# Three expert blocks: the first layer of 512 tokens from Strassen's products of 256, in place of plain matmuls of 512

## The chip, the cores and the metric

The kernel runs on 1 core of one Trainium2 chip. The metric is the device time of one execution in microseconds (us), as a median of runs. The core has five engines that work side by side: TensorE (PE, with the weight loads shown apart as PEld), VectorE (DVE), ScalarE (ACT), GpSimd (POOL) and SyncE (SP), which here only issues DMAs. PE writes its results into 8 PSUM banks.

## What is computed

Three layers in a row, on 2 x 576 = 1152 tokens of 512 features. The reference, cut to what matters here:

```python
scores = scale * q @ k.T + decay, causal; attn = softmax(scores); x = attn @ v   # B=2, H=8, S=576, D=64
p = domain_probs / domain_probs.sum(-1)
for e in range(4):                                # experts, 512 -> 1024 -> 512
    h = np.maximum(x @ w1[e], 0.0)
    out += p[:, e:e + 1] * (h @ w2[e])
h = out @ w_in                                    # MLP, 512 -> 2048 -> 512, weights in float64
return (h * (1.0 / (1.0 + np.exp(-1.702 * h)))) @ w_out
```

## The kernel before

Every fp32 matrix product is made of three matmuls in a faster 32-bit format: each operand is split into a rounded part (hi) and the rest (lo), and hi·hi, lo·hi and hi·lo are added in PSUM. The split of a weight tile (`split_w`, L212) is one operation on ACT (`whi`, through L60) and one on DVE (`wlo`, L230); the split of a result of the first layer is a relu and rounding on ACT and a subtraction on DVE or POOL.

The work is cut into visits: a visit is one block of 512 hidden units (blocks 0 to 7 are halves of the four experts, 8 to 11 quarters of the MLP) on some tokens. The list is made at L145 to L147. Visits 0 to 6 run beside attention on its chunks of tokens; visits 7 to 9 (from `v_exp`) are blocks 3, 1 and 0 on tokens 512 to 1151; visits 10 to 13 (from `v_all`) are blocks 4 to 7 on all tokens; visits 14 to 17 (from `v_mlp`) are the MLP's blocks. Tokens come in groups: `EXP[0]` and `EXP[1]` (E0 and E1 below) are two of 320 tokens, `REST` is the first 512, and `MLP` is three of 384.

The first layer (L1) of a visit has two forms. The plain one (`emit_l1`, kind 1 in the list `seq`) makes four groups of 12 matmuls, over all the group's tokens at once. The joint one (`emit_joint`, kind 3) takes two groups of tokens of the same size as the two columns of a 2 x 2 block product and needs 7 products instead of 8 (Strassen's scheme in Winograd's form), in two halves (m = 0 and 1) of 7 steps, each step one product of 6 matmuls with the moving size of one group. Its operands are sums of weights and of tokens that have splits of their own: `sum_weights` (L243, 4 operations on POOL of 256 columns), `high_sums` and `low_sums` (`sh` on ACT, `sl` on DVE, two of 512 columns each, or both in `split_sums`), and `sum_tokens` (L290) for E0 and E1 or the MLP's groups. A product's result is combined with others on DVE in `first_part` (ACT), `second`, `third`, `third_out`, `fourth`, `fifth`, `plain_out` and `plain_low` (L929 to L963); some of these outputs go through the tile `jc` (2 buffers), ACT's relu and rounding, and POOL's subtraction (`output`, L907). The product named s4 adds into the same bank that `third_out` reads. The second layer (L2, kind 2) makes one tile of 128 tokens per step, 12 matmuls of 512 columns, and DVE adds it to the accumulator (L1049). REST's second layer takes its tiles in the order 3, 0, 1, 2.

For blocks 4 to 7 the list gives, per visit: joint half E0, then L2 of REST of the visit before, joint half E1, L1 of REST (plain, kind 1, moving size 512), L2 of E0 (five tiles).

The order of the work is written out by hand in a loop over `seq` (L1228 to L1318). Each step emits its matmuls, then the evacuation of the step before, then due splits (`split_next`), then what `place` (L1190) has put at that step, then steps of the conversion of the MLP's weights, at a rate (`cv_due`, L1307). ACT, DVE and POOL are held to this order (`pin_turn`, L1141); PE is held to it only up to the joint halves of the first visit on all tokens (L1313), and otherwise may take what is ready. `place` places weight sums and splits for visits 8 to 10 only; for later visits the sums follow the splits of their own weights.

The MLP's weights come in float64. `mlp_convert` (L349) turns each of 32 tiles into float32 with one ACT and six DVE operations, one per step of the generator (192 steps); SP stores each to DRAM (`wm`), and SP loads them again in pairs for `split_w`. The weights of the second layer use two pools of four buffers in turn (`wb_p` and `late["wb"]`).

## Time and profile before

| | us |
|---|---|
| median of 3 runs | 692.34 (692.19 to 693.61) |
| the profiled execution, whole | 693.89 |
| its span, first to last instruction | 692.2 |
| busy in it: PE / PEld / DVE / ACT / POOL | 681.9 / 596.3 / 505.4 / 341.7 / 222.3 |

The rows further down come from the one profiled execution. A timeline row gives the start, the time of the row, the engine, the line of the kernel, the operation, and what it writes and reads; x4 says that four like instructions are drawn together. The time of one matmul in a row holds its way through the array, so that rows overlap; what a matmul costs in a stream is the distance from start to start. Where an engine was idle before an instruction, the brackets give for how long and what ended it.

### The profile page before, as it was taken

How to read it: one execution, taken by the hardware profiler on the slowest of the kernel's cores; microseconds unless marked ns; L12 is line 12 of the kernel's file. 1: busy time of each engine (PE TensorE's matmuls, PEld its weight loads, DVE VectorE, ACT ScalarE, POOL GpSimd, SP SyncE). 2: the span in 40 equal slices, each digit the busy share in tenths (PEclk: the TensorE clock that was granted, in tenths of full speed). 3: DMA queues.
4: the chain of work that ended last, by engine and by line, in shares of the span. 5: the costliest groups of instructions: out<-in, count | busy, mean ns of one | idle time of the engine just before them, and what ended most of it. 6: DMA issues, size and time to landing. Idle time of an engine off the chain costs nothing.

```text
span 692.2 us, 10730 instructions
## 1 busy us (share of the span) xinstructions
PE 681.9 (99%) x3829; PEld 596.3 (86%) x3829; DVE 505.4 (73%) x1057; ACT 341.7 (49%) x789; POOL 222.3 (32%) x266
## 2 busy tenths in 40 slices
PE   8998999999999999999999999999999999999997
PEld 4787888888988998898888888888899998998986
DVE  6886677766569678686876788777699798786632
ACT  5768677666532735734334344343457462551420
POOL 6877576532133554515105114112004202200000
PEclk9999999999999999999999999999999999999999
DMA  7696636341312144142422452344132244221012
GB/s 258 224 303 236 232 122 242 92 118 73 104 48 65 58 122 147 52 137 78 140 103 82 148 152 78 121 152 143 56 107 76 77 157 158 81 93 45 1 46 91
DMA packets 38597, 83.37 MB, mean 120 GB/s; under 512 B 3560, under 2 KB 3568, under 8 KB 38544
## 3 DMA queue, kind: packets, MB, share of 16 engines
q1 hardware_dynamic: 38504, 82.65, 36.1%
q8 instruction: 30, 0.49, 0.3%
q14 instruction: 23, 0.19, 0.1%
q10 hardware_dynamic: 40, 0.04, 0.0%
HBM read 71.88 MB, written 10.78 MB: 119 GB/s over the span
## 4 chain that ended last, share of the span: by engine, by line
PE 94%; DMA 2%; POOL 1%; DVE 1%; ACT 1%; issue 0%; SPq 0%; POOLq 0%; ACTq 0%
PE m L1016 43%; PE m L866 20%; PE m L904 19%; PE s L587 4%; PE x L691 4%; PE t L661 3%; DMA wst<-in_wa_moe_dram 1%; PE m L1161 1%; DMA dpraw<-in_dp_dram 1%; POOL ks L513 0%; PE m L883 0%; POOL e L643 0%; PE t L735 0%; PE m L1077 0%; POOL qlo L531 0%
## 5 line engine op out<-in xcount | busy, mean ns | idle before, releaser
L1016 PE MATMUL m<-whi,hh 128*128 128x512 f32 x432 | 121.7, 392 | 0.0
L1016 PE MATMUL m<-whi,hl 128*128 128x512 f32 x432 | 119.6, 390 | 0.0
L1016 PE MATMUL m<-wlo,hh 128*128 128x512 f32 x432 | 119.2, 390 | 0.0
L230 DVE TENSOR_TENSOR wlo<-wst,whi 128x512 fp32r<-128x512 f32 x140 | 105.2, 767 | 7.6 <-ACT whi L60 7.1
L1016 PEld LDWEIGHTS m<-wlo,hh 128*128 128x128 f32 x432 | 80.9, 188 | 16.9
L1016 PEld LDWEIGHTS m<-whi,hl 128*128 128x128 f32 x432 | 80.9, 188 | 16.8
L60 ACT ACTIVATE whi<-wst 128x512 fp32r<-128x512 f32 x144 | 85.4, 625 | 17.3 <-DMA wst<-in_wa_moe_dram 7.4
L1016 PEld LDWEIGHTS m<-whi,hh 128*128 128x128 f32 x432 | 79.5, 188 | 13.9
L914 POOL TENSOR_TENSOR hl<-jc,hh 128x320 fp32r<-128x320 f32 x42 | 39.6, 945 | 156.5 <-ACT hh L60 151.6
L251 POOL TENSOR_TENSOR sr<-wst 128x256 f32<-128x256 f32 x20 | 18.1, 903 | 150.0 <-DVE tl L306 47.8
L866 PE MATMUL m<-xh,whi 128*128 128x256 f32 (+2 forms) x304 | 64.3, 327 | 0.3 <-DVE hl L1005 0.3
L866 PE MATMUL m<-xh,wlo 128*128 128x256 f32 (+2 forms) x304 | 64.3, 325 | 0.0
L866 PE MATMUL m<-xl,whi 128*128 128x256 f32 (+2 forms) x304 | 63.9, 326 | 0.0
L643 POOL TENSOR_SCALAR e<-e,sm 128x128 f32<-128x128 f32 (+4 forms) x72 | 45.5, 642 | 54.9 <-DVE sm L641 29.0
L912 ACT ACTIVATE jc<-jc 128x320 f32<-128x320 f32 x42 | 19.7, 469 | 75.3 <-DVE jc L910 75.3
L1049 DVE SCALAR_TENSOR_TENSOR acc<-m,dpn,acc 128x512 f32<-128x512 f32 x63 | 46.6, 744 | 11.0 <-PE m L1016 11.0
L866 PEld LDWEIGHTS m<-xh,whi 128*128 128x128 f32 x304 | 50.4, 189 | 3.8 <-DVE hl L1005 0.6
L866 PEld LDWEIGHTS m<-xh,wlo 128*128 128x128 f32 x304 | 50.6, 189 | 2.5
L866 PEld LDWEIGHTS m<-xl,whi 128*128 128x128 f32 x304 | 50.2, 189 | 2.6
L633 ACT ACTIVATE e<-e,mx 128x128 f32<-128x128 f32 (+4 forms) x72 | 41.6, 581 | 12.2 <-DVE mx L617 11.5
L999 ACT ACTIVATE m<-m 128x384 f32<-128x384 f32 x48 | 23.0, 479 | 35.6 <-DVE m L910 33.1
L931 ACT ACTIVATE u<-m 128x320 f32<-128x320 f32 (+1 forms) x20 | 9.0, 451 | 62.7 <-PE m L904 62.7
(141 smaller groups left out, 1326.3 us busy)
## 6 DMA issues: line engine op xcount, KB each, us to landing
wst<-in_wa_moe_dram SPq DMA_DIRECT2D x28, 512.0 KB, 3.7
wst<-in_wb_moe_dram SPq DMA_DIRECT2D x28, 512.0 KB, 4.2
mst<-in_wa_mlp_dram SPq DMA_DIRECT2D x16, 512.0 KB, 4.0
wm<-wf SPq DMA_DIRECT2D x32, 256.0 KB, 3.4
mst<-in_wb_mlp_dram SPq DMA_DIRECT2D x16, 512.0 KB, 3.8
wst<-wm SPq DMA_DIRECT2D x16, 512.0 KB, 3.6
cb<-cumd SPq DMA_DIRECT2D x16, 256.0 KB, 3.9
qr<-in_qk_dram SPq DMA_DIRECT2D x8, 384.0 KB, 5.2
```

What stands on the lines that cost most here:

```text
L60: return nc.scalar.activation(out=out, in_=in_, func=AF.Copy)
L230: (nc.gpsimd if v_ == 0 and kind == 'a' and g < 4 else nc.vector).tensor_sub(lf, raw, f(hf))
L587: nc.tensor.matmul(pt[:, :z - a], lhsT=lr[i][0], rhs=lr[i][1], start=i == 0 and not (both and pt is not bank), stop=i == n - 1, skip_group ...
L633: nc.scalar.activation(out=e[:, off:off + w], in_=e[:, off:off + w], func=AF.Exp, scale=-1.0, bias=mx, accum_out=sm[:, 0, k:k + 1])
L643: nc.gpsimd.tensor_scalar(out=e[:, off:off + w], in0=e[:, off:off + w], scalar1=sm[:, 0, i:i + 1], scalar2=1.0, op0=ALU.mult, op1=ALU.mult)
L691: nc.tensor.matmul(pt[64 * g:64 * g + 64, o:n], lhsT=lhsT, rhs=rhs, start=i == 0, stop=i == nk - 1)
L866: nc.tensor.matmul(p[:, :n], lhsT=w[:, k, :], rhs=x[c][:, k, :], start=(j == 0 and k == 0), stop=(j == 2 and k == 3))
L904: nc.tensor.matmul(p[:, :WN], lhsT=w[a][:, k, :], rhs=x[z][:, k, :], start=start and j == 0 and k == 0, stop=stop and j == 2 and k == 1, s ...
L914: nc.gpsimd.tensor_sub(hl[:, g, :], r, f(hh[:, g, :]))
L999: nc.scalar.activation(out=p[:, :n], in_=p[:, :n], func=AF.Gelu_apprx_sigmoid)
L1016: nc.tensor.matmul(p, lhsT=h_tile(v_, b, c, j, x, k), rhs=wb[v_, k][w].rearrange("p a c -> p (a c)"), start=i == 0 and k == 0, stop=i == 2 ...
L1049: nc.vector.scalar_tensor_tensor(out=a, in0=p, scalar=d, in1=a, op0=ALU.mult, op1=ALU.add)
```

## The change

For blocks 5, 6 and 7 (`both_joint`, visits 11 to 13) REST's first layer is made by the joint form too, on chunks 0 and 1 of the attention, 256 tokens each (unit kind 7, two halves of 7 steps). The order in these visits becomes E0, L2 of REST of the visit before, 7/0, E1, 7/1, L2 of E0. The token sums for this are made and split during attention (`rest_sums`, three steps of a generator per step of the main loop), stored to DRAM, and loaded into the memory of the second pool of second-layer weights in block 4 (`load_rest_sums`, on POOL's queue); the second-layer weights of blocks 4 to 11 then have one pool. The joint form gets two orders of its evacuations (`tight`, `held`), and E1's half the order of products that visits 7 to 9 use in it. Weight sums, their splits and the weights' splits are placed at fixed steps for visits 11 to 13, PE is held to program order in them, REST's L2 goes through its tiles in the order 0, 1, 2, 3, and the conversion has other rates: none in joint units, 2 to 3 a step in L2 units, and 1.75 instead of 1.3 in the MLP.

```diff
+    both_joint = range(v_all + 1, v_mlp)
...
+        if v_ in both_joint:
+            seq += [(3, v_, b, cs[0])] + before + [(7, v_, b, 0), (3, v_, b, cs[1]), (7, v_, b, 1), (2, v_, b, cs[0])]
+            before = [(2, v_, b, REST)]
+            continue
...
-        p = wa_p if kind == "a" else late["wb"] if late and v_ % 2 else wb_p
+        p = wa_p if kind == "a" else wb_p
...
-    placed = range(v_exp + 1, v_all + 1)
+    placed = range(v_exp + 1, v_mlp)
...
+    def rest_sums():
...
+        def split(n, r, o):
+            t = room.tile([128, 2, SA], F32R, tag="rs", name="rs")
+            round_act(t[:, 0], r)
+            yield
+            nc.vector.tensor_sub(t[:, 1], r, f(t[:, 0]))
+            yield
+            nc.sync.dma_start(out=tsd[:, :, n - 1, o].rearrange("x p n -> p x n"), in_=f(t))
+            yield
...
+        for o in range(2):
+            yield from total(ra, o, (sub_, h12, h11), (add_, ra, l12), (sub_, ra, l11))
+            yield from split(1, ra, o)
+            yield from total(rb, o, (sub_, h22, ra), (add_, rb, l22))
+            yield from split(2, rb, o)
+            yield from total(ra, o, (sub_, rb, h21), (sub_, ra, l21))
+            yield from split(4, ra, o)
+            yield from total(rb, o, (sub_, h22, h12), (add_, rb, l22), (sub_, rb, l12))
+            yield from split(3, rb, o)
...
+    def load_rest_sums():
+        for t, src in zip(tsr, tsd):
+            nc.gpsimd.dma_start(out=t, in_=src.rearrange("p n k c -> p n (k c)"))
...
-    def emit_joint(v_, b, m):
-
-        c1, c2 = visits[v_][1][:2]
+    held = []
+
+    def emit_joint(v_, b, m, ts, c1, c2):
+
         WN = span[c1][1]
-        late_sums = m == 1 and len(visits[v_][1]) == 2
+        tight = v_ in both_joint and (c1 == 0) != m
+        late_sums = m == 1 and (v_ < v_all or v_ in both_joint and c1 == EXP[0])
...
+                while held:
+                    held.pop()()
...
-                yield both_(third_out, fourth)
+                yield third_out if tight else both_(third_out, fourth)
                 product(pa, a12, ts[21], False, True)
-                yield both_(plain_out, plain_low)
+                yield both_(plain_out, fourth if tight else plain_low)
...
-                yield both_(fourth, plain_low)
+                yield fourth if tight else both_(fourth, plain_low)
             product(pc, s4, ts[22], False, True)
-            yield fifth
+            yield both_(fifth, plain_low) if tight else fifth
...
-        if c == REST:
-            j = (3, 0, 1, 2)[j]
...
+        for v_ in range(v_all, v_mlp):
+            b, (c1, c2, _) = visits[v_]
+            h0, h1, l2 = (3, v_, b, c1), (3, v_, b, c2), (2, v_, b, c1)
+            more = v_ + 1 in both_joint
+            if v_ == v_all:
+                mid = (1, v_, b, REST)
+                put(h1, 0, load_rest_sums)
+                put(h0, 1, sum_weights, v_ + 1, 0)
+                put(mid, -0.5, high_sums, v_ + 1, 0)
+                put(mid, 0, low_sums, v_ + 1, 0)
+                put(mid, 1, sum_weights, v_ + 1, 1)
+                continue
+            r0, r1 = (7, v_, b, 0), (7, v_, b, 1)
+            put(r0, 5.5, high_sums, v_, 1)
+            put(h1, -0.5, low_sums, v_, 1)
+            if more:
+                put((2, v_ - 1, b - 1, REST), 2, sum_weights, v_ + 1, 0)
+                put(h1, 1, sum_weights, v_ + 1, 1)
+                put(r1, 6, high_sums, v_ + 1, 0)
+                put(l2, 0, low_sums, v_ + 1, 0)
+            fill = (2, v_ - 1, b - 1, REST)
+            for k, (u, i) in enumerate([(fill, 3), (fill, 3), (r0, 0), (r0, 1)]):
+                put(u, i, split_w, "b", v_, k)
+            for g in range(4):
+                put(l2, g, split_w, "a", v_ + 1, g)
...
+            if rest_gen and not late:
+                for _ in range(3):
+                    next(rest_gen[0], None)
...
-                    cv_due[0] += ((0.75 if kind == 4 else 0) if v_ < v_all else 1.4 if b < NMOE else 1.3) * (4 / n_steps)
+                    if v_ in both_joint and v_ + 1 in both_joint or v_ + 1 == v_mlp and c != REST or v_ == v_all and kind == 2 and c == REST:
+                        rate = 0 if kind != 2 else 11 / 4 if c == REST else 2
+                    elif v_ == v_all:
+                        rate = {3: 0, 1: 1.25, 2: 3.25}[kind]
+                    else:
+                        rate = (0.75 if kind == 4 else 0) if v_ < v_all else 1.4 if v_ == v_all else 1.75
+                    cv_due[0] += rate * (4 / n_steps) if rate != 11 / 4 else 3 * (g < 3)
...
-                pinned = v_ < v_all or v_ == v_all and kind == 3
+                pinned = v_ < v_all or v_ == v_all and kind == 3 or v_all <= v_ < v_mlp and u in pin_units
```

## Rows read from the trace of the kernel before

**Rows 1.** The page: busy time and share by engine; the last chain by engine.

```profile
PE 681.9 (99%) x3829; PEld 596.3 (86%) x3829; DVE 505.4 (73%) x1057; ACT 341.7 (49%) x789; POOL 222.3 (32%) x266
...
PE 94%; DMA 2%; POOL 1%; DVE 1%; ACT 1%; issue 0%; SPq 0%; POOLq 0%; ACTq 0%
```

**Rows 2.** Busy time by windows: attention's last part, blocks 5 to 7, the MLP.

```profile
core 0: us, PE busy (x) PEld busy (x) DVE busy (x) ACT busy (x) POOL busy (x), PEclk, DMA share, GB/s
140.00:200.00 60.00, 60.00 (x416) 51.27 (x415) 34.81 (x103) 35.30 (x97) 14.98 (x26) 1.00 0.28 91
200.00:217.30 17.30, 17.30 (x89) 15.72 (x88) 16.78 (x24) 6.06 (x11) 6.14 (x6) 1.00 0.19 62
337.80:480.80 143.00, 143.00 (x720) 124.50 (x719) 108.65 (x204) 54.77 (x119) 34.66 (x38) 1.00 0.37 122
510.00:650.00 140.00, 140.00 (x706) 126.92 (x705) 112.97 (x192) 67.63 (x136) 19.75 (x20) 1.00 0.27 92
```

**Rows 3.** Timeline, PE: starts of matmuls of 256, 320 and 512 columns.

```profile
131.60 0.64 PE L866 MATMUL m<-xl,whi 128*128 128x256 f32 x4
...
133.52 0.39 PE L1016 MATMUL m<-whi,hh 128*128 128x512 f32 x1
...
339.54 0.46 PE L904 MATMUL m<-th,sh 128*128 128x320 f32 x2
...
341.30 0.46 PE L904 MATMUL m<-th,whi 128*128 128x320 f32 x2
...
373.76 1.07 PE L1016 MATMUL m<-whi,hl 128*128 128x512 f32 x4
...
376.48 0.39 PE L1016 MATMUL m<-whi,hl 128*128 128x512 f32 x1
```

**Rows 4.** Groups by line and shape: busy us, mean ns | idle before.

```profile
L1049 DVE SCALAR_TENSOR_TENSOR acc<-m,dpn,acc 128x512 f32<-128x512 f32 x63 | 46.6, 744 | 11.0 <-PE m L1016 11.0
L914 POOL TENSOR_TENSOR hl<-jc,hh 128x320 fp32r<-128x320 f32 x42 | 39.6, 945 | 156.5 <-ACT hh L60 151.6 <-issue 4.8
L251 POOL TENSOR_TENSOR sr<-wst 128x256 f32<-128x256 f32 x20 | 18.1, 903 | 150.0 <-DVE tl L306 47.8 <-DVE sl L266 38.7 <-DMA wst<-wm 23.6
L1005 DVE SCALAR_TENSOR_TENSOR hl<-m,hh 128x256 fp32r<-128x256 f32 x32 | 13.5, 421 | 6.0 <-ACT hh L1004 5.5
L934 DVE TENSOR_TENSOR u<-m,u 128x320 f32<-128x320 f32 x14 | 6.8, 484 | 3.6 <-issue 2.6 <-ACT hh L60 0.7 <-PE m L904 0.2
```

**Rows 5.** Timeline, POOL: weight sums one behind the other.

```profile
281.90 0.74 POOL L251 TENSOR_TENSOR sr<-wst 128x256 f32<-128x256 f32 x1
282.61 0.73 POOL L252 TENSOR_TENSOR sr<-wst 128x256 f32<-128x256 f32 x1
```

**Rows 6.** Timeline: hand-overs from PE to DVE, and a late sum's split.

```profile
341.50 0.49 DVE L937 TENSOR_TENSOR u<-m,u 128x320 f32<-128x320 f32 x1
...
347.59 1.09 PE L1016 MATMUL m<-wlo,hh 128*128 128x512 f32 x4
347.85 1.16 ACT L60 ACTIVATE sh<-sr 128x512 fp32r<-128x512 f32 x2 [2.60 <-PE m L904]
...
348.51 1.29 DVE L266 TENSOR_TENSOR sl<-sr,sh 128x512 fp32r<-128x512 f32 x2 [3.87 <-ACT sh L60]
...
359.41 1.28 DVE L230 TENSOR_TENSOR wlo<-wst,whi 128x512 fp32r<-128x512 f32 x2
```

**Rows 7.** Waits: engine, line, what ended them; total us, times, longest.

```profile
PEld m L904 <- DVE sl L284: 0.2, 1, 0.2
```

**Rows 8.** DMA issues: the store and the reload, KB each, median us to landing.

```profile
wm<-wf SPq DMA_DIRECT2D x32, 256.0 KB, 3.4
...
wst<-wm SPq DMA_DIRECT2D x16, 512.0 KB, 3.6
```

**Rows 9.** Timeline, DVE: two of the conversion's six operations.

```profile
340.22 0.68 DVE L368 SCALAR_TENSOR_TENSOR wf<-mst,cvt 128x512 uint32<-128x512 uint32 x1
...
340.94 0.43 DVE L371 TENSOR_SCALAR cvt<-wf 128x512 uint32<-128x512 uint32 x1
```

More of the change, by code (lines that the diff above doesn't have):

```diff
@@ L36, with __init__, __getitem__ @@
 WARM, FILL = 11, (4, 3, 3, 2, 2, 2, 3, 3,)
+class Halves:
+    def __init__(self, *parts):
+        self.parts = parts
+    def __getitem__(self, at):
+        p, k, n = at
+        return self.parts[k // 2][p, k % 2, n]
 @with_exitstack
@@ L216, in split_w @@
         raw = raw_w.pop((kind, v_, g))
-        p = wa_p if kind == "a" else late["wb"] if late and v_ % 2 else wb_p
-        hi = p.tile([128, 4, 128], F32R, tag="hi", name="whi")
-        lo = p.tile([128, 4, 128], F32R, tag="lo", name="wlo")
+        p = wa_p if kind == "a" else wb_p
+        if kind == "b" and v_ in (v_exp, v_exp + 2):
+            hi, lo = (t[:, g].rearrange("p (a c) -> p a c", a=4) for t in tsr)
+        else:
+            hi = p.tile([128, 4, 128], F32R, tag="hi", name="whi")
+            lo = p.tile([128, 4, 128], F32R, tag="lo", name="wlo")
         hf = hi.rearrange("p a c -> p (a c)")
@@ L424, in begin_late, with view @@
         late["cd"] = pool("cd", 1)
[L425 removed]
+        late["wb"] = pool("wb2", 1)
         late["rs"] = pool("rs", 1)
[L427 removed]
+        h2 = tuple(late["h2"].tile([128, 4 * WN], F32R, name=n) for n in ("hh2", "hl2"))
+        def view(ts_, o, k, n):
+            return tuple(t[:, o:o + k * n].rearrange("p (k n) -> p k n", k=k) for t in ts_)
+        hbuf[0] = view(h2, 0, 4, WN)
+        rest_h.append(view(h2, 0, 4, SA))
+        rest_h.append(tuple(Halves(*t) for t in zip(view(h2, 4 * SA, 2, SA), view(h_t, 8 * JN, 2, SA))))
+        tsr.extend(late["wb"].tile([128, 4, 512], F32R, name=n) for n in ("tsh", "tsl"))
         acc.append(late["rs"].tile([128, 4, 512], F32, name="acc1"))
@@ L914, in output @@
                 nc.gpsimd.tensor_sub(hl[:, g, :], r, f(hh[:, g, :]))
+            if b >= NMOE:
+                evac_l1(v_, b, c, g, r)
+            elif hold:
+                held.append(rest)
             else:
-                evac_l1(v_, b, c, g, r)
+                rest()
         def half(m):
@@ L923, in half @@
             if late_sums:
-                pa, pc, _, pe, pb, pd = (ps_tile() for _ in range(6))
+                pa, pc = ps_tile(), ps_tile()
+                if v_ < v_all:
+                    ps_tile()
+                pe, pb, pd = (ps_tile() for _ in range(3))
+                if v_ >= v_all:
+                    pb, pc = pc, pb
             else:
@@ L1173, in steps @@
             return len(tiles(c)) - OVER
-        return {1: 4, 2: len(tiles(c)), 3: 7, 4: 10 - OVER, 5: OVER, 6: OVER}[kind]
+        return {1: 4, 2: len(tiles(c)), 3: 7, 4: 10 - OVER, 5: OVER, 6: OVER, 7: 7}[kind]
     split_q = []
     def split_next():
+        if late and not lo_due and pair_due:
+            pair_due.pop()()
         split_rest()
@@ L1223, in attn_moe_mlp @@
     place_at = place()
+    pin_units = [u for u in seq if u[1] in both_joint and (u[1], u[3]) != (v_mlp - 1, REST)] + [u for u in seq if u[:2] == (2, v_all) and u[3] == REST]
     evac = [lambda: None]
     j_done = set()
+    rest_gen, rest_from = [], seq.index((1,) + units[6])
     cv_due = [0]
@@ L1234, in attn_moe_mlp @@
             ts_gen = sum_tokens(EXP)
-        u, m = (kind, v_, b, c), visits[v_][1].index(c)
+        if i >= rest_from and not late and ready[0] >= 1:
+            rest_gen.append(rest_gen.pop() if rest_gen else rest_sums())
+        u, m = (kind, v_, b, c), c if kind == 7 else visits[v_][1].index(c)
         if u == (1, v_mlp, NMOE, MLP[0]):
```

57 lines of the change are left out of this document (35 added, 22 removed).

## The prediction

> **What bounds the kernel now.** I read the page's busy times and its chain by engine first: PE is busy for 681.9 of 692.2 us and holds 94% of the chain that ended last [rows 1]. Then the windows: the stretch that holds blocks 5, 6 and 7 (337.8 to 480.8, from E0's half of block 5 on) is filled by PE to the last hundredth, 143.00 us at a granted clock of 1.00, while DVE has 34 us free there, ACT 88 and POOL 108 [rows 2]. So less matmul time there is less time, one for one, unless PE meets a wait that it doesn't have now. The stages on both sides, attention's last part (140 to 217.3) and the MLP (510 to 650), are filled by PE in the same way [rows 2]. DVE work moved there is free as long as DVE's free share lasts: 25 us in the 60 up to 200, 0.5 in the 17.3 behind, 27 in the MLP's 140.
>
> **What it removes: matmul time.** The price of a matmul is the spacing of starts. 12 of 512 columns take 376.48 - 373.76 = 2.72 us, 226.8 ns each; 12 of 320 take 341.30 - 339.54 = 1.76 us, 146.6 ns; 16 of 256 take 133.52 - 131.60 = 1.92 us, 120.0 ns [rows 3]. That is 0.417 ns a column and 13.4 ns fixed. The first layer of REST is now 4 x 12 = 48 matmuls of 512: 10.89 us. In the new form it is 14 products of 6 matmuls of 256: 84 x 0.120 = 10.08 us. Saved: 0.81 us a block, 2.42 us for three. The columns alone (24576 against 21504) would give 1.28 us a block; 36 more starts take 0.48 back.
> The Trainium skill says in Perfetto Trace Analysis, Optimizing Tensor Performance, Matmuls, that larger matmuls are more efficient than smaller ones. That speaks against this change, and the trace agrees by the fixed part of each start; by the rows it takes a third of the gain and not all of it.
>
> **What it adds between the products.** Each block gets 8 outputs combined from products in the place of four plain evacuations, and its weight sums and splits sit at fixed steps. Durations: a DVE add of 320 columns from PSUM 0.485, an operation of 256 0.42; POOL's subtraction of 320 0.94 (0.76 of 256 by the same ratio); an accumulation 0.74 [rows 4]; a POOL weight sum 0.74 with starts 0.71 apart when little runs beside it [rows 5]; a wlo 0.60 behind the one before (two in 1.28), a DVE add 0.20 behind the last matmul it reads [rows 6]. I put these, with the change's new order, into each engine's queue: DVE, ACT and POOL are held to program order now, and with the change PE is too in these blocks, so that no other matmul can fill a PE wait. Walking the queues of 7/0 (the first new half), E1 and 7/1 gives three waits.
> (A) The last product of 7/0, s4, adds into the bank that third_out reads, and must wait for it. It is due after six products, 6 x 0.72 = 4.32 us. On DVE stand, from the half's start: an accumulation of the L2 before (0.2 to 0.86), three wlo (2.66), second, the fourth wlo (3.6), third (4.06), third_out (4.48); with some 0.13 to PE that is 4.61: 0.3 late, three blocks: 0.9 us. Bounds 0 (one wlo less ahead of it) and 1.8 (one more short operation).
> (B) The s3 product of 7/1, in blocks 5 and 6, needs the PSUM bank that E1's plain_low gives back. From E1's start: the block's own late sums on ACT, then their two sl on DVE, which end 2.2 us behind (as now: PE begins the next work at 347.59, the second sl ends at 349.80 [rows 6]); fifth of 7/0 on DVE to 2.5, its relu and rounding on ACT to 3.4, its subtraction on POOL to 4.2; then the four weight sums of the next block, 7.1; then the subtraction of E1's third_out, 8.0. The tile jc has two buffers, so E1's fifth waits for that subtraction and ends at 8.5, plain_low at 9.0, PE starts at 9.1. It could start at 7 x 0.88 + 0.15 (wait C) + 3 x 0.72 = 8.5. 0.62 late, two blocks: 1.24 us. Queued behind that waiting fifth on DVE are plain_low, second and third. Bounds 0.4 and 1.4 a block (each sum and subtraction 0 to 0.15 longer).
> (C) E1's s4 waits for its third_out too. Its first_part stands on ACT behind the relus that 7/0 left and ends 3.7 us behind E1's start; second, third and third_out follow at 0.53 each, 5.30, and PE at 5.43; due 6 x 0.88 = 5.28. 0.15 late, three blocks: 0.45 us. Bounds 0 and 0.9.
> Such a wait is seen once now: a weight load waits 0.2 us for an sl [rows 7]. Sum of the waits 2.59 us; bounds 0.8 (B's lower end alone) and 5.5.
>
> **What it moves.** (D) REST's token sums go into attention: 44 steps, which are 28 DVE operations (x 0.42 = 12 us), 8 on ACT (3 us) and 8 stores on SP's queue from one buffer, each some 3.4 us as those of wm [rows 8]. They go three to a step while DVE has 25 us free in 60 [rows 2]; each of the 8 parts must wait for the store before it (about 8 x 4.4 = 35 us in all). If that takes them past 200, they meet a DVE that is 97% busy [rows 2]. On DVE, what waits behind them is attention's own softmax work. I take 0.2 us; bounds 0 and 1.
> (E) Loading them back is two DMAs on POOL's queue, 1 MB each, where POOL is busy for a quarter of the time and the first reader is some 30 us away: 0; 1 us if their issue held up the subtractions behind it.
> (F) The second layer's weights, with one pool where two were, are split at 7/0's first steps, behind the last L2 of the block before, which frees them. The splits are in walk A; their loads come a block ahead. 0.
> (G) REST's L2 now ends on tile 3, which the MLP's first work doesn't read: its first L1 group, 48 matmuls of 384 (0.417 x 384 + 13.4 = 173 ns each), covers the transposition for 8.3 us. 0.
> (H) Conversion of MLP weights: by the two sets of rates 85 of its 192 steps lie ahead of the MLP, where 121 do now. 36 steps of 0.55 us (half of them 0.68, half 0.43 [rows 9]) = 20 us of DVE go into the MLP's 140 us, where DVE is busy for 113 [rows 2]: 133, or 95%. A key is stored (3.4 us) and loaded again (3.6 us) before it is split [rows 8]. At the new rate, seven steps a unit where it was 5.2, the nearest case is the second pair of the fourth MLP block's first weights: its last key is made as the third block's last first-layer work begins, and its split comes 6.2 us later against 7.0. ACT, half free, would stand 0.8 us, and PE's banks hold longer than that: 0; bounds 0 and 8.
>
> **Sum.** The profiled execution is 693.89; the median of the runs, 692.34, is 1.55 lower. 693.89 - 2.42 + 2.59 + 0.2 = 694.26 for a profiled one, 692.7 as a median: the waits between the products take back what the products save.
>
> **Rivals.** This measurement can tell about 0.2%, 1.4 us, from no change.
> (1) The waits don't arise: the walk is 0.3 us too slow in DVE's queue (A and C vanish with that) and POOL takes the two subtractions before the sums, or ends them sooner (B falls to 0.4). The time is 692.34 - 2.42 + (0 to 0.8) + 0.2 = 690.1 to 690.9. For it: A and C are smaller than the error of a queue walk; blocks 5 to 7 have almost no wait today [rows 7]; DVE is a quarter free [rows 2]. Against: six products of 256 last 4.3 us where those of 320 last 5.3, with the same operations between. Chance 0.33.
> (2) Converted MLP weights come late (H). It decides at one key: if the one named there is finished one conversion later (six steps and their gaps, about 4 us), ACT stands in the split's wait with gelu and rounding queued behind it, the banks stay full, and PE loses 2 to 8 us: 695 to 700 with the rest of the sum. For it: DVE at 95%. Against: ACT is half free, and the walk has the key in time to within a microsecond. Chance 0.12.
> (3) POOL's sums run beside DVE at their mean and not at their best: 0.90 against 0.74 [rows 4, 5]. Four sums and two subtractions then end 0.85 us later in B, twice, and the time is 692.7 + 1.7 = 694.4, slower by 0.3%. It decides by what DVE does in those 3 us: with two SBUF operands (a wlo, an sl) it slows them, with PSUM operands (second, third, as beside the sums of 281.90) it doesn't. By the walk it is the latter. Chance 0.10, together with (D) at its upper bound.
> The Trainium skill, SBUF — State Buffer, SBUF: two separate sides, says that a DVE operation with two SBUF inputs and a POOL operation that reads SBUF lock each other out for the whole instruction. The two means bear out that something lengthens the sums; that it is whole instructions they don't show, 0.16 us being a quarter of one wlo.
>
> **How the numbers follow.** Forecast: 692.7, its own range 691.0 to 693.7, chance 0.45 (no change by over 0.2%). Faster by over 0.2%, rival 1: 0.33. Slower by over 0.2%, rivals 2 and 3: 0.22. The range goes from rival 1 with a little to spare, 689.8 (what the products save, with no wait and 0.1 for a start or two) to 695.5 (all waits at their upper bounds: 692.34 - 2.42 + 5.5 + 0.2 = 695.6). Rival 2's upper part is left out.
>
> **What would show it.** In the profile after: 256-wide products of L904's successor 120 ns apart, 84 in 10.1 us; PE or its weight loads waiting for third_out's add 0.1 to 0.4 us in 7/0 and E1, and for E1's plain_low 0.6 us in 7/1 of blocks 5 and 6; DVE 12 us busier in 140 to 217 without a PE gap; DVE near 133 in the MLP's 140 us, and no wait of ACT over 1 us for a wst loaded from wm. Wrong for rival 1 if PE keeps going in blocks 5 to 7, and for rival 2 if the MLP's stretch is over 1 us longer.

## The result: 7.6 us slower, and the profile after

The changed kernel takes 700.24 us (median of 4 runs, 698.43 to 701.09) against 692.67 of the kernel before beside it: a ratio of 1.0104, 95% interval 1.008 to 1.0128. The prediction was 692.7 with a range up to 695.5; the time lies outside it, on the slower side. The profiled execution's span is 698.9 us (692.2 before), its own time 700.62.

Of the page after, the line that answers to [rows 1], busy time and share by engine:

```profile
PE 684.1 (98%) x3937; PEld 600.5 (86%) x3937; DVE 533.3 (76%) x1097; ACT 352.8 (50%) x821; POOL 235.0 (34%) x286
```

PE has 108 matmuls more, as the 84 for 48 ask, and should have been busy for 2.4 us less; it is busy for 2.2 us more and idle for 4.5 more. DVE is busy for 28 us more. Where it went is read from the starts of the same work in both timelines (the first matmul of each piece):

| start of | before | after | later by |
|---|---|---|---|
| the first joint half (block 3, E0) | 217.32 | 220.02 | 2.70 |
| block 5, E0 | 337.79 | 340.31 | 2.52 |
| block 6, E0 | 385.55 | 387.96 | 2.41 |
| the first joint MLP unit | 537.54 | 539.90 | 2.36 |
| the second MLP joint visit | 585.13 | 587.46 | 2.33 |
| the third | 632.69 | 638.02 | 5.33 |
| end of the span | 692.2 | 698.9 | 6.7 |

So attention loses 2.7, the three blocks that the change is about gain 0.16 in all (2.52 to 2.36), and the MLP loses 4.3. The windows after (columns as in [rows 2]): a stretch of attention, blocks 5 to the first joint MLP unit, and from there to the end.

```profile
90.00:100.00 10.00, 7.96 (x41) 6.81 (x40) 9.59 (x30) 4.97 (x16) 8.23 (x11) 0.83 0.43 143
...
340.30:539.90 199.60, 198.97 (x1129) 179.29 (x1128) 151.79 (x258) 91.62 (x196) 52.03 (x60) 1.00 0.28 88
...
539.90:698.90 159.00, 152.43 (x757) 135.82 (x755) 118.61 (x216) 62.14 (x126) 14.47 (x16) 1.00 0.35 115
```

The same stretches in the kernel before:

```profile
90.00:100.00 10.00, 10.00 (x64) 9.01 (x63) 6.36 (x27) 6.72 (x22) 9.03 (x12) 1.00 0.37 118
...
337.80:537.50 199.70, 199.70 (x1021) 175.91 (x1020) 156.66 (x277) 85.49 (x176) 42.72 (x46) 1.00 0.34 111
537.50:692.20 154.70, 151.08 (x757) 136.25 (x756) 101.80 (x181) 59.37 (x121) 11.70 (x13) 1.00 0.24 83
```

In the ten us from 90 on PE is empty for 2.0 us, the granted clock falls to a mean of 0.83, and DVE goes from 6.36 to 9.59 busy. The timeline there (DVE and POOL, and PE where it starts again):

```profile
90.25 2.56 POOL L596 TENSOR_TENSOR qlo<-qr,qhi 64x384 fp32r<-64x384 f32 x2
91.95 1.14 DVE L362 TENSOR_TENSOR rsa<-rsa,xl 128x256 f32<-128x256 f32 x1
92.88 1.46 POOL L578 TENSOR_TENSOR ks<-kq,ks 64x576 fp32r<-64x576 f32 x1
93.01 1.62 DVE L355 TENSOR_TENSOR rs<-rsb,rs 128x256 fp32r<-128x256 f32 x1
94.88 0.14 DVE L705 TENSOR_SCALAR sm<-sm 128x1 f32<-128x1 f32 x1
...
95.01 1.22 PE L1099 MATMUL m<-whi,hh 128*128 128x512 f32 x2 [2.04 <-DVE sm L705]
```

L355 and L362 are REST's token sums (L355 the subtraction of their split). The loop emits them from 147 us on; the compiler has put them between 58 and 128. With POOL idle such an operation takes 0.41; here two take 1.14 and 1.62, and the short softmax step `sm`, queued behind them, is what PE waits for.

In 7/0, E1 and 7/1 of block 6 (DVE, POOL and PE):

```profile
409.15 0.42 DVE L980 TENSOR_TENSOR jc<-m,u 128x256 f32<-128x256 f32 x1
...
409.63 0.51 PE L974 MATMUL m<-xh,sh 128*128 128x256 f32 x2
...
415.42 0.49 DVE L980 TENSOR_TENSOR jc<-m,u 128x320 f32<-128x320 f32 x1
...
415.97 0.56 PE L974 MATMUL m<-xh,sh 128*128 128x320 f32 x2
...
417.53 1.71 POOL L985 TENSOR_TENSOR hl<-jc,hh 128x320 fp32r<-128x320 f32 x2
...
418.44 0.49 DVE L980 TENSOR_TENSOR jc<-m,u 128x320 f32<-128x320 f32 x1 [2.13 <-POOL hl L985]
418.85 0.48 DVE L1045 SCALAR_TENSOR_TENSOR hl<-m,hh 128x320 fp32r<-128x320 f32 x1
419.10 0.40 PE L974 MATMUL m<-tsh,sh 128*128 128x256 f32 x2
```

Waits A and C are there: third_out ends at 409.57, s4 starts at 409.63, 0.30 behind the end of the product before it; in E1 the same, 0.24. For wait B, the fifth of E1 does stand on DVE for 2.13 us behind POOL and plain_low ends only at 419.33, but the s3 product starts at 419.10 without waiting, while plain_low (418.85) still runs.

And in the MLP (ACT, DVE and PE; PE had no such wait there before):

```profile
603.69 0.51 PE L974 MATMUL m<-xl,sh 128*128 128x384 f32 x2
604.29 1.15 ACT L71 ACTIVATE sh<-sr 128x512 fp32r<-128x512 f32 x2 [3.63 <-PE m L974]
604.96 1.29 DVE L285 TENSOR_TENSOR sl<-sr,sh 128x512 fp32r<-128x512 f32 x2 [4.53 <-ACT sh L71]
604.98 1.14 PE L974 MATMUL m<-th,sh 128*128 128x384 f32 x4 [0.78 <-ACT sh L71]
...
643.23 0.67 ACT L418 ACTIVATE cvt<-mst 128x512 f32<-128x512 f32 x1 [9.27 <-DMA mst<-in_wb_mlp_dram]
643.80 0.47 ACT L1012 ACTIVATE u<-m 128x384 f32<-128x384 f32 x1
644.33 0.62 PE L974 MATMUL m<-xh,whi 128*128 128x384 f32 x2 [0.92 <-ACT u L1012]
```

PE waits for a late sum's split and for first_part (`u`), which stands on ACT behind a conversion's first operation that waits 9.27 us for its load.

### The profile page after: what moved, and what is told of

It is laid out like the page before. It is cut to its first block, busy times and chain, and to the rows that moved or that the text cites. A ratio compares the mean times of both kernels' runs of the same rounds, so it can differ in the third digit from the quotient of the medians.

```text
span 698.9 us, 11089 instructions
## 1 busy us (share of the span) xinstructions
PE 684.1 (98%) x3937; PEld 600.5 (86%) x3937; DVE 533.3 (76%) x1097; ACT 352.8 (50%) x821; POOL 235.0 (34%) x286
## 5 line engine op out<-in xcount | busy, mean ns | idle before, releaser
L1099 PE MATMUL m<-whi,hh 128*128 128x512 f32 x392 | 109.9, 395 | 2.6 <-DVE sm L705 2.0
L1099 PE MATMUL m<-wlo,hh 128*128 128x512 f32 x392 | 108.2, 393 | 0.0
L1099 PE MATMUL m<-whi,hl 128*128 128x512 f32 x392 | 106.7, 390 | 0.0
L985 POOL TENSOR_TENSOR hl<-jc,hh 128x320 fp32r<-128x320 f32 (+1 forms) x60 | 53.4, 891 | 144.6 <-ACT hh L71 141.4
L983 ACT ACTIVATE jc<-jc 128x320 f32<-128x320 f32 (+1 forms) x60 | 27.1, 451 | 58.9 <-DVE jc L980 58.8
L934 PE MATMUL m<-xh,wlo 128*128 128x256 f32 (+2 forms) x256 | 51.4, 314 | 0.0
L934 PE MATMUL m<-xh,whi 128*128 128x256 f32 (+2 forms) x256 | 51.1, 316 | 0.0
L934 PE MATMUL m<-xl,whi 128*128 128x256 f32 (+2 forms) x256 | 50.9, 315 | 0.0
L934 PEld LDWEIGHTS m<-xl,whi 128*128 128x128 f32 x256 | 41.1, 189 | 0.7
L418 ACT ACTIVATE cvt<-mst 128x512 f32<-128x512 f32 x32 | 21.3, 665 | 31.3 <-DMA mst<-in_wb_mlp_dram 17.4
```

Of the source, the lines that this page charges most:

```text
L418: nc.scalar.activation(out=f(t), in_=f(hi), func=AF.Abs)
L934: nc.tensor.matmul(p[:, :n], lhsT=w[:, k, :], rhs=x[c][:, k, :], start=(j == 0 and k == 0), stop=(j == 2 and k == 3))
L983: nc.scalar.activation(out=r, in_=r, func=AF.Relu)
L985: nc.gpsimd.tensor_sub(hl[:, g, :], r, f(hh[:, g, :]))
L1099: nc.tensor.matmul(p, lhsT=h_tile(v_, b, c, j, x, k), rhs=wb[v_, k][w].rearrange("p a c -> p (a c)"), start=i == 0 and k == 0, stop=i == 2 ...
```

## The experiments

Times are medians, with the kernel before at 692.85 to 693.23 beside them. The two theories: S, the token sums' place and work cost attention its 2.7 us; C, the conversion steps moved into the MLP cost it its 4.3 (4.4 in the expectations). The rivals stand in the expectations.

**e1: sums held to the loop's order.**

```diff
-                    next(rest_gen[0], None)
+                    in_turn(next, rest_gen[0], None)
```

> The new kernel, with REST's token sums held to the place where the loop puts them (after 147 us) on DVE and ACT; nothing else. In the new kernel the trace has them between 58 and 128 us, some of them 1.1 to 1.6 us long, and PE is empty for 2.0 us at 93 us waiting for DVE, then runs at a lower granted clock for some us; joint work begins 2.7 us later than before (220.02 against 217.32). Theory S (the place of the sums costs attention its time): joint work begins at 217.3 to 217.8, the time falls by 2 to 3 us, to 697 to 698.5. Rival (the 12 us of DVE work or the 8 stores cost it wherever they stand): joint work begins at 219 or later, and the time stays at 699 to 701.

Measured: 699.76 (ratio 1.0096, 1.0081 to 1.0111). The gap at 93 us is gone. The first joint half starts at 216.1, but nine matmuls of 512 (2.04 us), which stood ahead of it, stand behind it in this version, so its start can't be set beside 217.32 and 220.02. The second visit's can: 247.5, against 246.1 before and 248.8 after. The sums now end at 202 us, and from 200 to 250 PE doesn't wait. Its one long wait is earlier:

```profile
180.72 0.38 SPq L357 DMA_DIRECT2D tsd<-rs  x1
181.15 1.00 SPq L77 DMA_DIRECT2D wst<-in_wb_moe_dram  x2
...
186.34 1.15 ACT L71 ACTIVATE whi<-wst 128x512 fp32r<-128x512 f32 x2 [1.91 <-DMA wst<-in_wb_moe_dram]
...
187.02 1.02 PE L1099 MATMUL m<-whi,hh 128*128 128x512 f32 x3 [1.26 <-ACT whi L71]
```

PE waits for a weight split on ACT, and ACT for its load. SP issues that load right behind a store of the sums, which needs their split on DVE; that the store held it up is read from this order and not tried alone. Both are half right: the compiler's place cost a gap, but 1.4 of the 2.7 us stay in the loop's place too.

What the gap costs hangs on the clock too. In the profiles of the changed kernel and of e6, e7 and e8 the granted clock falls behind the gap, and the first joint half starts at 220.0 to 221.6; in e2, e4, e9 and e18, with gaps of 1.6 to 2.0 us at the same place and no fall, it starts at 217.7 to 218.5. So some 1.5 of the 2.7 us go with the fall.

**e2 and e3: the conversion as before, alone and with e1.**

```diff
-                    if v_ in both_joint and v_ + 1 in both_joint or ...
+                    if v_ < v_all:
+                        rate = 0.75 if kind == 4 else 0
+                    elif b < NMOE:
+                        rate = 1.4 if v_ == v_all else {3: 1.4, 7: 0, 2: 2.1}[kind]
+                    else:
+                        rate = 1.3
+                    cv_due[0] += rate * (4 / n_steps)
```

> The new kernel, with about as many conversion steps ahead of the MLP as before (121 instead of 85) and 1.3 instead of 1.75 in the MLP; REST's Strassen units still get none. Theory C (the 36 steps moved into the MLP fill DVE there and make PE wait): the stretch from the first MLP joint unit to the end falls from 159.0 to 154.7 us as before, and blocks 5 to 7 get 0 to 1 us longer by the steps in E0 and E1; 695.5 to 697. Rival (the MLP's loss comes from the single pool of second-layer weights or from PE's new order): 699 to 701.

> Both edits: sums in turn, conversion steps as before. If theories S and C are both right and are all of the loss, the losses of 2.7 and 4.4 us go and what is left is the joint blocks' own account (saved 2.42, waits of about 1.8): 691.5 to 693.5. If either is wrong it stays above 695.

Measured: 705.44 (1.018, 1.0162 to 1.0198) and 704.64 (1.0168, 1.0148 to 1.0189), slower than the change. The windows of e2, blocks 5 to the first joint MLP unit and from there on:

```profile
340.00:548.30 208.30, 202.15 (x1130) 182.28 (x1129) 165.27 (x286) 94.18 (x200) 56.42 (x63) 0.98 0.34 104
548.30:702.90 154.60, 150.98 (x757) 136.22 (x755) 102.33 (x182) 59.52 (x121) 12.88 (x14) 1.00 0.25 84
```

The MLP has its 154.6 us back, as C says, and the blocks lose 8.7 against the 199.6 after. That no theory had. PE in e2's timeline, s4 in E1 (blocks 5, 6) and in 7/0 (block 7):

```profile
370.31 0.90 PE L974 MATMUL m<-xh,sh 128*128 128x320 f32 x2 [2.33 <-DVE jc L980]
...
420.73 0.56 PE L974 MATMUL m<-xh,sh 128*128 128x320 f32 x2 [1.52 <-DVE jc L980]
...
463.92 0.51 PE L974 MATMUL m<-xh,sh 128*128 128x256 f32 x2 [2.01 <-DVE jc L980]
```

These are waits A and C, grown from 0.3 to 2: the conversion's operations stand ahead of third_out. PE stands for 6.2 us of this stretch (0.6 in the changed kernel), 5.9 of them in these three waits; the other 3.2 us are the same matmuls lasting longer (202.15 us busy, 198.97 in the changed kernel), and the granted clock falls behind two of the waits (0.74 and 0.83 in 368 to 376, 0.94 and 0.64 in 462 to 470, each over 4 us). So the steps were not free to stay where they were; moving them is part of what the Strassen form costs.

**e4: four load buffers in the MLP instead of two.**

```diff
+            j = m_loaded[0] % 4
+            t = m_extra[j - 2] if m_extra and j > 1 else late["st"].tile(...)
...
+            mx = late["wb"].tile([128, 2, 1024], U32, tag="tsh", name="mx")
+            m_extra.extend((mx[:, 0], mx[:, 1]))
```

> The new kernel, with four buffers instead of two for the loaded float64 weights from the MLP's start on (two of them in the memory of REST's token sums, which is free by then). It tells how DVE's load reaches PE. In the new kernel ACT stands 7.2 and 9.3 us in a conversion's first operation, waiting for such a load, with first_part behind it, and PE then waits 0.9 us for first_part. Theory C1 (the link is that wait on ACT): those waits go, and the time falls by 1.5 to 3 us, to 697.2 to 698.7. Theory C2 (DVE's own queue is late, whatever ACT does): within 0.7 us of the new kernel, 699.5 to 701.

Measured: 698.47 (1.009, 1.0068 to 1.0111), which by the ratio is 1.0 us under the change and inside its interval. In the profile the waits of ACT for a load are gone and so is the 0.92 us at 644, and the MLP's stretch is 157.8 instead of 159.0. C1 is one of the links, worth about 1 of the 4.3 us; PE's other three waits of over half a us stay (0.78 for `sh`, 0.71 and 0.55).

**e5 and e6: each part alone, in the kernel before.**

```diff
-... else 1.4 if b < NMOE else 1.3) * (4 / n_steps)
+... else 0.95 if b < NMOE else 1.75) * (4 / n_steps)
```

> One part alone, in the kernel before: its conversion steps are moved as the change moves them (0.95 a unit-quarter instead of 1.4 in blocks 4 to 7, which leaves about 85 of 192 ahead of the MLP, and 1.75 instead of 1.3 in the MLP). No Strassen for REST, no new sums. Theory C (the moved conversion steps alone cost the MLP its 4.4 us): blocks 5 to 7 as in the kernel before (no gap to fill), the stretch from the first joint MLP unit to the end 157.5 to 160 instead of 154.7, the time 695 to 698. Rival (the MLP's loss comes from the single weight pool, or another order of PE, that this kernel does not have): 692 to 694.

> The other part alone, in the kernel before: REST's token sums are made and stored during attention as in the change (nothing reads them). Theory S: joint work begins 2 to 3 us later (219.3 to 220.5 against 217.3), the time is 694.5 to 696. Rival (the 2.7 us in the changed kernel come from something else, such as the memory taken from attention or the compiler's new order): 692 to 694.

Measured: e5 699.28 (1.0088, 1.0073 to 1.0103) and e6 696.34 (1.0043, 1.0031 to 1.0055). In e5 the MLP's stretch takes 159.8 us, 5.1 more than before, with the same waits, 0.78 for `sh` and 0.79 for `u`; blocks 5 to 7 are as before. In e6 the first joint half starts at 220.2, and the gap is the same one:

```profile
95.13 1.20 PE L1048 MATMUL m<-whi,hh 128*128 128x512 f32 x4 [2.03 <-DVE sm L672]
```

Each part alone costs its stage about what the whole change costs it there, without any of the new Strassen products: 5.1 where the change has 4.3, and 2.9 where it has 2.7. (The medians are 6.3 and 3.3 above the kernel before, more together than the change's 7.6, so the parts don't add up exactly.) S and C hold as causes; the Strassen products, the single weight pool and the held order of blocks 5 to 7 are not needed for either. The order that the compiler gives PE in the MLP isn't out: it differs from the order before at 298 of 756 matmuls in the changed kernel and at 270 in e5.

**e7: the MLP's low weight parts on POOL.**

```diff
-            (nc.gpsimd if v_ == 0 and kind == 'a' and g < 4 else nc.vector).tensor_sub(lf, raw, f(hf))
+            (nc.gpsimd if v_ == 0 and kind == 'a' and g < 4 or v_ >= v_mlp else nc.vector).tensor_sub(lf, raw, f(hf))
```

> The new kernel, with the low parts of the MLP's weights (32 subtractions of 512 columns) made on POOL instead of DVE. It takes some 20 us off DVE in the MLP, about what the 36 moved conversion steps put there, and leaves those steps. Theory C (DVE's queue): the stretch from the first joint MLP unit to the end falls from 159.0 to 154.5 to 156.5, the time to 696 to 698. Rival C1 (only the wait for the loads of the conversion matters): 699 to 701. It gets worse, 701 or more, if POOL's 1.27 us an operation, with the weight sums behind it, becomes the late part, or if POOL and DVE slow one another.

Measured: 704.21 (1.0156, 1.0139 to 1.0174), worse. The groups of e7 (busy us, mean ns):

```profile
L249 POOL TENSOR_TENSOR wlo<-wst,whi 128x512 fp32r<-128x512 f32 x36 | 52.8, 1479 | 123.7 <-ACT whi L71 123.6
...
L433 DVE TENSOR_TENSOR wf<-wf,cvd 128x512 f32<-128x512 f32 x32 | 29.5, 922 | 0.5
```

L433 had a mean of 739 ns in the changed kernel. DVE's 32 subtractions are gone, and DVE is busy for 121.82 of 162.40 us where it was 118.61 of 159.00: what remained got longer by as much. The operation was moved, not the load.

**e8: one wlo less ahead of third_out.**

```diff
-... [(fill, 3), (fill, 3), (r0, 0), (r0, 1)]
+... [(fill, 3), (fill, 3), (r0, 0), (r0, 5)]
```

> The new kernel, with the split of the fourth second-layer weight tile put five steps after the first in 7/0 instead of one, so that one wlo less (0.60 us of DVE) stands ahead of third_out. Wait A (third_out is late because of DVE's queue): the 0.29 to 0.30 us ahead of s4 in 7/0 go to below 0.1 in blocks 5 to 7, and blocks 5 to 7 are 0.6 to 0.9 us shorter; time 699 to 699.7. Rival (third_out is bound by its chain second, third, third_out behind the products, not by the queue): no change, 700.2.

Measured: 700.19 (1.0105, 1.009 to 1.0121), no change. The wait in 7/0 is gone, as A says, and stands in E1 instead, 0.6 us in each block by the spacing of the starts (here block 5, where the row shows 0.42 of it):

```profile
368.63 0.56 PE L974 MATMUL m<-xh,sh 128*128 128x320 f32 x2 [0.42 <-DVE jc L980]
```

The moved split's ACT operation (362.72, 0.62 us) stands ahead of the late sums' `sh`, and with it sl, fifth, first_part and E1's third_out are later. The queue's cause was right, the gain wasn't: A turned into a larger C.

**e9: a smaller dose of moved steps.**

```diff
-                        rate = 0 if kind != 2 else 11 / 4 if c == REST else 2
+                        rate = 1.75 if (kind, c) == (3, EXP[0]) else 0 if kind != 2 else 11 / 4 if c == REST else 2
...
-                        rate = (0.75 if kind == 4 else 0) if v_ < v_all else 1.4 if v_ == v_all else 1.75
+                        rate = (0.75 if kind == 4 else 0) if v_ < v_all else 1.4 if v_ == v_all else 1.5
```

> The new kernel with a smaller dose of moved conversion steps: 7 of them go back into E0's half of each of blocks 5 to 7 (21 in all, so that some 106 of 192 lie ahead of the MLP), and the MLP's rate falls from 1.75 to 1.5. E0 is the joint half behind which the second layer of REST stands (10.9 us), not a Strassen half of 256. Theory C with the deadlines of e2 (steps hurt where a product follows within 4 to 5 us and waits for an output on DVE: E1 and 7/0; elsewhere DVE catches up): blocks 5 to 7 longer by at most 0.5 us in all, the MLP (first joint unit to the end) 155.5 to 157.5 instead of 159.0, time 697 to 699. Rival (any step in these blocks is late in the end, as all pass through one queue): blocks 5 to 7 longer by 2 us or more, time 700 or above.

Measured: 694.90 (1.0032, 1.0022 to 1.0042), 5.3 us under the change and better than expected. The windows of e9, the MLP and the blocks:

```profile
537.60:692.20 154.60, 150.96 (x757) 136.20 (x755) 108.73 (x196) 60.52 (x123) 11.99 (x15) 1.00 0.30 99
338.00:537.60 199.60, 198.95 (x1130) 179.32 (x1129) 160.84 (x278) 94.08 (x199) 53.41 (x62) 1.00 0.33 103
```

All 4.3 us are back, and the blocks pay nothing. The rest of the 5.3 isn't the MLP's: attention, which this edit leaves alone, happens to be 2.3 us shorter in e9's profile than in the changed kernel's (the first joint half at 217.69; the clock doesn't fall there). With 108.73 us of DVE in the MLP nothing is lost, with 117.85 (e5) 5.1. C holds, and in these three versions its price isn't in proportion to the work but sets in between 70% and 74% of DVE. Moved steps cost nothing in E0 and, left in the joint halves, 1.5 to 2.3 us a half ahead of third_out (e2).

**e10, e11, e12: other places for the sums.**

```diff
-        sub_, add_ = nc.vector.tensor_sub, nc.vector.tensor_add      # e10, e11
+        sub_, add_ = nc.gpsimd.tensor_sub, nc.gpsimd.tensor_add
...
-    rest_gen, rest_from = [], seq.index((1,) + units[6])              # e10, e11, e12, with in_turn as in e1
+    rest_gen, rest_from = [], seq.index((1,) + units[5])
```

> The new kernel, with REST's token sums made on POOL instead of DVE (28 operations of 256 columns, 0.74 us or more each), held to the loop's place, and begun one unit earlier (some 126 us). POOL is busy for 3 to 10 us in each 20 there. Theory S (DVE's share of the sums is what costs attention and the joint work behind it): the second visit's joint work, 248.8 in the new kernel, 247.5 in e1 and 246.1 before, comes at 246 to 247, time 697 to 698.5. Rival (POOL's softmax steps, queued behind the sums, are late instead, or POOL and DVE slow one another): 248.5 or later, time 700 or more.

> The three edits together: sums on POOL, the smaller dose of moved steps, four load buffers. If each acts on its own stage, the gains add: 2 from the sums, 2 from the dose, 1 from the buffers, 695 to 696. It would be under the kernel before (693) only if all the loss is in those two places, which the blocks' own account (0.1 to 0.2 us gained a block) hardly allows.

> The new kernel with the sums on DVE in the loop's order as in e1, but begun one unit earlier (126 us instead of 147), so that they are over by some 180 us and not at 202, ahead of the stretch in which DVE is 97% busy with the token sums of E0 and E1. Theory S (they cost what they push into that stretch): the second visit's joint work at 246 to 247 instead of 247.5, time 697.5 to 699. Rival (12 us of DVE work on attention's path cost it wherever they stand): 247.5 or later, 699.5 to 700.5.

Measured: e10 703.15 (1.0154, 1.0139 to 1.0169), e11 699.05 (1.0096, 1.0076 to 1.0116), e12 699.10 (1.0095, 1.0078 to 1.0112). On POOL, where e10 puts the subtraction of their splits too, the sums take 0.73 to 0.90 us each, PE is held up at 182 us by ACT's weight split and softmax copy (1.0 and 0.8), and the second visit starts at 250.4: worse than any place on DVE. e11 is e9 with that loss. e12 starts the second visit at 246.9, 0.6 better than e1; its median is 0.7 lower, inside the intervals.

**e13 to e17: what of the sums costs, and what is left.** e13 is e9 with e12's edit. e14 is e9 with the 36 operations left out and the stores kept, e17 with the stores gone too; e15 makes the sums in block 4, e16 adds the old order of tiles to it.

```diff
+                for x, t in enumerate((h, l)):                        # e14, in the place of the sums
+                    nc.sync.dma_start(out=tsd[x, :, n, o], in_=f(t[:, o]))
...
+            nc.gpsimd.dma_start(out=t[:, n - 1].rearrange(...), in_=x[n - 1])      # e17, in block 4
...
+            if u == (1, v_all, visits[v_all][0], REST) and g == 1:    # e15, e16
+                rest_gen.append(rest_sums())
...
+        if c == REST:                                                 # e16
+            j = (3, 0, 1, 2)[j]
```

> The smaller dose of moved steps (e9) together with the sums on DVE in the loop's order from 126 us on (e12). If the two losses are apart, e12's gain of 1 us adds to e9's 5.3: 693.5 to 694.2. If the sums cost what they cost wherever they stand in attention: 694.9 as e9.

> As e9, with the token sums themselves left out: what the stores and the load carry is the tokens' own tiles, so REST's Strassen products are made from other operands. The same bytes go out and come back; the 28 DVE and 8 ACT operations are gone. If those operations are what costs attention: joint work begins at 216 to 217.4 as before, and the time is 691.7 to 692.7. If the stores on SP's queue (or the memory) cost it: 694 to 695.

> As e9, with the sums in block 4 in the place of conversion steps there (14 DVE operations and 4 on ACT, of 512 columns, straight into the tiles that the products read, no store and no load), two steps of them per step of the loop; the conversion steps displaced go to blocks 3, 1 and 0 (1.75 instead of 0.75), some 107 of 192 ahead of the MLP. If both costs of the change are places and not work: attention as before, blocks 5 to 7 gain their 0.1 to 0.2 us each, the MLP as before: 691.5 to 692.7, at or a little below the kernel before. If DVE's work in block 4 or in blocks 3, 1 and 0 is then late: 693.5 to 695.

> As e15, with the old order of REST's L2 tiles (3, 0, 1, 2). From the last block's E0 to the MLP's first matmuls the new kernel gained 0.45 us and lost 0.5 behind them, up to the first joint MLP unit. If that loss is the order of the tiles: 0.3 to 0.6 us below e15. If not: within 0.3 us of it.

> As e9, with the token sums and their stores left out: in block 4 eight copies on POOL's queue bring the tokens' own tiles to the place of the sums, so REST's Strassen products are made from other operands. Attention then has nothing of the change in it. The Strassen blocks' own account: 2.42 saved, waits ahead of s4 of about 0.6 a block measured, the rest of the kernel as before: 692.0 to 692.6 where the kernel before has 692.9. If stores cost something in e14 (693.7), this is 0.7 to 1.5 lower than e14; if they cost nothing, it is 693.5 as e14.

Measured: e13 695.19 (1.0034, 1.0023 to 1.0045), as e9: in attention no place that was tried makes the sums cheaper than some 2 us. e14 693.74 (1.001, 1.0001 to 1.0019), e17 692.68 (0.9997, 0.9988 to 1.0006). Both together cost e9 2.2 us. The operations are worth 1.2 of it; the stores seem to be worth the rest, but the intervals of e14 and e17 overlap, so their share isn't shown. In e17 the ten us from 90 on are as before, PE full and DVE at 5.83:

```profile
90.00:100.00 10.00, 10.00 (x63) 8.84 (x63) 5.83 (x27) 6.12 (x22) 6.76 (x10) 1.00 0.35 115
336.60:536.30 199.70, 199.06 (x1130) 179.32 (x1130) 160.89 (x277) 94.09 (x199) 53.40 (x63) 1.00 0.33 103
```

e15 709.92 (1.0244, 1.0221 to 1.0267) and e16 709.73 (1.0226, 1.0197 to 1.0255): attention is as before (217.6, 216.0), but against e17 the visits of blocks 1 and 0, with the displaced conversion steps, last 1.2 and 3.8 us longer, and blocks 4 and 5, with the sums and conversion steps, 4.2 and 8.0: PE waits for third_out's add there (block 4, then block 5's E0).

```profile
310.97 0.56 PE L965 MATMUL m<-xh,sh 128*128 128x320 f32 x2 [2.28 <-DVE jc L971]
...
357.40 0.90 PE L965 MATMUL m<-xh,sh 128*128 128x320 f32 x2 [3.36 <-DVE jc L971]
```

e16 against e15: all starts from the first joint half on are earlier by the same 1.61 to 1.66 us, so the tiles' order costs nothing (G).

**e18: PE free to choose in blocks 5 to 7.**

```diff
-                pinned = v_ < v_all or v_ == v_all and kind == 3 or v_all <= v_ < v_mlp and u in pin_units
+                pinned = v_ < v_all or v_ == v_all and kind == 3
```

> As e9, with PE no longer held to program order in blocks 5 to 7. If the waits ahead of s4 (0.3 in 7/0, 0.24 in E1) stand only because PE may not take other work: they go, blocks 5 to 7 are 1 to 1.8 us shorter, 693.3 to 694. If the compiler's own order has nothing ready to put there, or splits the second layer's groups at a bad place: 694.7 to 697.

Measured: 708.24 (1.0223, 1.0208 to 1.0239), far worse: blocks 5 to the first joint MLP unit take 210.8 us instead of 199.6. The compiler puts halves of 256 and of 320 into one another, and PE then waits for the same outputs longer:

```profile
364.05 0.50 PE L974 MATMUL m<-xh,sh 128*128 128x256 f32 x2 [2.07 <-DVE jc L980]
...
415.91 0.80 PE L974 MATMUL m<-xh,sh 128*128 128x256 f32 x2 [2.45 <-DVE jc L980]
```

None of these versions beats the kernel before; the fastest that computes the sums is e9, 0.32% slower than it. e17, without them, is equal to it.

## Why the prediction was wrong, step by step

**The matmul time: right.** In block 5, 7/0 runs from 357.37 to 362.80 and 7/1 from 369.30 to 374.33: 5.03 us without a wait and 5.43 with A, against 42 x 0.120 = 5.04 in the prediction.

**The waits: nearly right in sum, one of three wrong.** A was put at 0.30 and is 0.30, with 0.1 more because the first matmuls behind it are slow; C was put at 0.15 and is 0.24, 0.34 with that. B was put at 0.62 and is 0: its whole chain came (fifth waits 2.1 us for POOL, plain_low ends at 419.33), but the bank that s3 needs was not that one. The step took the banks as given in turn, so that s3 gets the eighth before it. They aren't: in the program as built s3 gets in block 6 a bank that E1's `second` had read, and the one that plain_low reads goes to 7/1's sixth product, which starts only at 420.54. So B came to nothing because of a step that was wrong, and not because the chain was shorter. The prediction's net for the three blocks was 2.59 - 2.42 = 0.17 us lost; by the starts it is 0.16 gained in all, and e17, where nothing else of the change costs time, is 692.68 against 692.85. "The waits take back what the products save" holds, in part by luck: B's 1.24 us is missing, and some 0.9 of it comes back by a longer C and by the slow first matmuls behind A and C.

**D, the sums: the step that failed first.** They were put at 0.2 us, bounds 0 and 1; they cost attention 2.7 in the profile (some 1.5 of it with the fall of the clock), 3.3 in e6's median and 2.2 by e9 and e17. Two things in the step were wrong. It took DVE as held to program order, as the description of the kernel before says without a limit; that is so from visit 7 on. In attention the compiler orders DVE, and it put the sums between 58 and 128 us, where DVE had 4.5 to 7.3 us free in each 20 and not the 8.4 of the stretch from 140 to 200. And it priced an operation at 0.42, the row of a PSUM operation. The sums read two tiles of SBUF, and beside POOL took up to 1.62. The Trainium skill, SBUF — State Buffer, SBUF: two separate sides, has the rule: such an operation and a POOL operation that reads SBUF lock each other out, and the second waits for the first's end. The trace agrees here instruction by instruction: L362 ends at 93.09, 0.28 us behind POOL's L596 (92.81), and L355 at 94.63, 0.29 behind L578 (94.34). The prediction had said that the means didn't show this; they are means over operations of which most met none. The place isn't the whole cost either: held to the loop's (e1), the sums still cost 1.4.

**H, the moved conversion: rival 2, with the mechanism wrong.** The DVE work was sized about right (20 us said, 118.61 - 101.80 = 16.8 measured), and taken as free since DVE had 27 us left in 140. It cost 4.3 us, put at 0. Rival 2 had the place and a price of 2 to 8 us, but put it down to converted weights that come late, at one key; the only wait of ACT for a reload in the MLP's second half is 1.2 us. What the trace shows in its place are four waits of PE for short results of ACT and DVE, 2.95 of the 4.3 us. For `u` at 609.27 (0.70) and 644.33 (0.92) ACT has a conversion's first operation ahead, at 644 one that waited 9.27 us for a load, which was issued at 639.26, right behind the last read of its buffer. For `hl` at 622.23 (0.55) DVE has a wlo of 0.79 and conversion steps of 0.96 and 0.77 ahead. For `sh` at 604.98 (0.78) neither engine was behind: DVE had been idle for 4.53 us and ACT for 3.63. The split had to wait for the product that reads the tiles it overwrites (603.69), and the compiler had put this product behind second-layer matmuls. So by the trace DVE's and ACT's queues are a part, and PE's new order another; e5 shows waits of the same kinds in the kernel before. That a share of 74% of DVE costs this stage 5 us and 70% nothing (e5, e9) is the measured part; whether the waits would come with PE in its old order was not tried, and stays open.

**Rival 1** (no waits) wasn't the case: A and C stood in the blocks. **Rival 3** (sums beside DVE slow POOL): the sums in E1 took 0.73 to 0.74 each, as the prediction took them; its mechanism appeared elsewhere, in attention. **E, F, G:** the load's issue and the single pool show no wait of PE; G is settled by e16.

**The chances.** 0.22 for slower was too little: two costs that had been set at 0.2 and 0 because an engine had time left in a window came out at 2 to 3 and over 4 us, and the range's upper end took neither of them in.

## What to carry to other kernels

Free time of an engine in a window isn't room for more work on it when that engine's queue is in order and a short result for the bottleneck engine stands behind: price moved work by the deadline it stands ahead of, not by the window's share; here conversion steps cost nothing in E0, 1.5 to 2.3 us a half ahead of third_out, and 4.3 us in a stage where they took DVE to 75%. Moved work is part of the price of what it makes room for, and is best measured alone, in the kernel before. Before placing an operation at a line, find out whether its engine is held to program order there.

## What the runs showed of the hardware that was not expected

DVE operations on two SBUF tiles that started while POOL worked on SBUF ended 0.28 and 0.29 us behind POOL's end (91.95 and 93.01 us above). Moving half of such a pair to POOL made both longer: in e7 the means of DVE's conversion operations rose from 739 to 922 ns (L433) and POOL's own stood at 1479, where the four at the kernel's start take 1273.

A gap on PE can cost more than itself. The windows of the changed kernel around the one at 93 us (PE was busy for 3.82 of the 4 us up to 92, at 1.00, and then stood for 2.04 us):

```profile
88.00:92.00 4.00, 3.82 (x32) 3.39 (x31) 3.90 (x9) 3.16 (x8) 3.84 (x5) 1.00 0.11 34
92.00:96.00 4.00, 1.97 (x11) 1.60 (x10) 4.00 (x11) 1.42 (x5) 2.64 (x3) 0.86 0.52 158
96.00:100.00 4.00, 4.00 (x15) 3.26 (x14) 3.65 (x16) 2.32 (x10) 3.74 (x7) 0.71 0.53 194
```

The 0.86 and 0.71 are means over four us each: in the three windows of 1 us from 95 to 98 the granted clock is 0.50, the lower level, 1.2 GHz. Four matmuls of 512 take 1.58 us there (96.89 to 98.47 in the timeline), 0.40 each, where one takes 0.227 at 2.4 GHz. The length of the gap doesn't settle it: the clock fell behind gaps of 2.02 to 2.04 us at this place in the changed kernel, e6, e7 and e8, and stayed at 1.00 behind 2.02 in e2 and 2.01 in e4, as behind 1.72 in e9 and 1.60 in e18. What decides between them isn't shown here.
